# Making six of batch 1's products, and one group of tables, in an earlier step of a long-convolution and expert kernel

## The chip, the cores and the metric

The kernel runs on one core of a Trainium2 chip. The metric is the device time of one execution in microseconds. Three runs of the kernel before gave 3615.54, 3617.24 and 3617.27 us; their median, 3617.24 us, is the time before.

## What is computed

The first half is a Hyena filter: a small network gives a filter `h_filt` over 12480 positions and 128 channels, and every batch and channel of `u = x * v` is convolved with it by FFT. The second half is an expert block on every row of the result: two matrix products with `h * cos(h)` between them.

```python
h_filt = (np.maximum(pos_emb @ w1, 0.0) @ w2) * np.exp(-0.01 * pos)[:, None]
u = x * v                                  # x, v: (4, 12480, 128)
Uf = np.fft.rfft(u, n=2 * S, axis=1)
Hf = np.fft.rfft(h_filt, n=2 * S, axis=0)
y = np.fft.irfft(Uf * Hf[None], n=2 * S, axis=1)[:, :S, :]
attn = (x * y).reshape(49920, 128)
h = attn @ w_in                            # w_in: (128, 2048)
out = (h * np.cos(h)) @ w_out              # w_out: (2048, 128)
```

All inputs and outputs are float32, apart from the two expert weights, which are float64 and are converted on the chip.

## The kernel before

**The transform.** The convolution is done with matrix products: 11520 points are split as N1 = 96 times N2 = 120. For one batch there are five pieces of work, each written as a Python generator of *units*, which yields after each part of a unit, so that the pieces can be interleaved. The *products* (`u_units`) load x and v for two pairs of positions, multiply them (two instructions, L440, one for each half) and write the sum and the difference into `slots` (two instructions, L450): 30 units for a batch. The *forward step* (`f1_units`, L458 and its evictions L470) makes 64 matmul groups from `slots`. The *second step* (`f2_units`, and for the filter and batch 0 together `f2_both_units`) multiplies in the frequency domain. The *third step* (`i1_units`) makes the first half of the inverse, 64 units, each evicted from one of eight PSUM banks: mostly by an ACT copy (L562) and two DVE instructions (L564), and every eighth by an ACT copy (L555) and two POOL instructions (L558). The *last step* (`i2_units`) makes 30 groups of four positions, with a table tile `tm` for each group, multiplies by x (L586) and stores rows to `zd` in DRAM.

**The tables.** A group's tile is made by `make_group`, which calls `make_t` four times: an ACT copy with a factor (L329), another into one of two `spare` tiles (L334), and a POOL sum (L335); or, with a copy of the rows in PSUM, L329 and one DVE instruction (L331). Batch 0 makes its tiles itself and stores them in `td`, from where the later batches load them. The groups listed in `SOME` (2, 7, 12, 17, 22, 27) are made during the third step of batch 0 by `some_groups`, which also makes four sums of expert weights on POOL (L778) and at its end starts the last step, where group 0's tile is made.

**The order.** The program has two parts. Up to about 277 us the filter, batch 0's products, its forward, second and third steps run with nothing else on PE. Then the expert block runs, 98 tiles of 16 steps, and the rest of the convolution is threaded through it: `convolve` adds one step of credit for each step of the expert block and calls the generators until the credit is used up. During the last step of batch b the products of batch b + 1 are made (`inverse_units` calls `later_u_units`): L440 by POOL for one half and by DVE for the other, both L450 by POOL. Then come the forward, second and third steps of batch b + 1. The chain of the expert block for each step is PE (phase matmul, L138 `ph`), ACT (L870), DVE (L871), ACT (L876), DVE (L877); for each pair of steps POOL makes sums (L885, L888, L889), and PE multiplies by the output weights (L902).

Every engine runs its instructions in the program's order, and all DMAs of the program are issued on SP's queue, in order, each after its own waits. A tile of a pool has a number of buffers; a new tile waits until the one that had its buffer is no longer used.

The lines that matter in the third step of batch 0:

```python
with tc.tile_pool(name="ready", bufs=1) as pool:
    other = some_groups(pool)
    for i, _ in enumerate(i1_units(bank, lambda b: b % 8 == 3)):
        if i > 10 and i % 7 in (0, 3):
            next(other, None)
    for _ in other:
        pass
```

Just before this the weights (`w_in_sb`, `w_out_sb`, 1024 KB each) are loaded.

Of the kernel before, what the change touches and what calls it, by code (L numbers as in the profile page):

```python
# [10 lines left out]
F32 = mybir.dt.float32  # L11
# [3 lines left out]
ALU = mybir.AluOpType  # L15
# [19 lines left out]
def kernel(  # L35
# [46 lines left out]
    nc = tc.nc  # L82

    B, S, D = x.shape
# [3 lines left out]
    R = S // N2  # L88
    M = N1 * N2
    TURN = 4 * M  # L90
    H = N2 // 2
    ODD = 64
# [7 lines left out]
    CB = D // 2  # L100
# [5 lines left out]
    UA = 2  # L106
    NG = N2 // G
# [4 lines left out]
    ALONE = 8  # L112
    XV = 36
    LATER = 96
    AT = NFC // 2 + 2
    WCOL = 256

    dram = ctx.enter_context(tc.tile_pool(name="dram", bufs=1, space=DRAM))
# [3 lines left out]
    td = dram.tile([N2 // G, N1, G, 2, R], F32, name="td")  # L122
    wind = dram.tile([D, DFF], F32, name="wind")
    woutd = dram.tile([P, NFC // 2, 4 * CB], F32, name="woutd")
    csd = dram.tile([N2, 2, N2], F32, name="csd")
    rowsd = dram.tile([N1, 4, R], F32, name="rowsd")
    twd = dram.tile([N1, 2, N2], F32, name="twd")
# [297 lines left out]
    def clear_gap(u):  # L425

        nc.gpsimd.memset(u[:, :, H:ODD, :], 0.0)

    def u_load(place, b, a):
        tiles = []  # L430
        for i, src in enumerate((x, v)):
            tiles.append(place(a // UA, i))
            load_pairs(tiles[i], src, b, H - UA - a, H + a)
        return tiles

    def u_multiply(tiles, half, engine):
        xt, vt = (t[:, half] for t in tiles)
        if len(vt.shape) > len(xt.shape):
            xt = xt.rearrange("p (n d) -> p n d", n=UA)
        engine.tensor_tensor(xt, xt, vt, op=ALU.mult)  # L440
# [159 lines left out]

    def units(n, steps, before, mm, after, parts, ahead=2, skip=0):


        for j in range(min(ahead, n)):
            for _ in before(j) or ():
                pass
        yield 0.0
        last = iter(())  # L610
        for j in range(n):
            early = iter(before(j + ahead) or () if j + ahead < n else ())
            now = None
            for i in range(parts):
                if i == skip or 2 * (i - skip) == max(parts, 2):
                    now = mm(j, now, int(i > skip))
                if i == 0 and parts == 1:
                    now = mm(j, now, 1)
                next(last, None)
                next(early, None)  # L620
                yield steps / parts
            for _ in early:
                pass
            next(last, None)
            last = after(j, now)
        for _ in last:
            pass
        yield REST

    SOME = range(2, NG, 5)  # L630
    REST = 3.0
    U_STEPS, F1_STEPS, F2_STEPS, I1_STEPS, I2_STEPS = 2.0, 1.0, 3.4, 0.8, 1.5
    FIRST_STEPS, I2U_STEPS = 3.5, 3.4

    def u_units(b, u, engine, place, ahead, takers):

        tiles = {}

        def before(j):
            tiles[j] = u_load(place, b, j * UA)  # L640

        def after(j, _):
            for half in range(2):
                u_multiply(tiles[j], half, engine(j, half))
                yield
            if j == H // UA - 2:
                clear_gap(u)
            u_sums(u, tiles.pop(j), j * UA, takers(j))
            yield

        return units(H // UA, U_STEPS, before, lambda j, ps, i: None, after, 3, ahead=ahead)

    def later_u_units(b, u, engine, side):

        with tc.tile_pool(name="xv", bufs=3, side=side) as pool:
            def place(j, i):
                t = pool.tile([R, 2, UA * D], F32, name="xv"[i] + "t", bufs=3 - i)
                return t[:, :, :]

            yield from u_units(b, u, engine, place, 1, lambda j: (nc.gpsimd, nc.gpsimd))  # L660

    def f1_units(bank, u, share, evict=f1_evict):
        def mm(j, ps, i):
# [106 lines left out]
    def some_groups(pool):  # L770
        for g in SOME:
            t = pool.tile([N1, G, 2, R], F32, name="some", bufs=2)
            yield from make_group(pool, g, t, G)
            if g == SOME[2]:
                for dst, first_, second_, op in ((4, 1, 3, ALU.add), (5, 4, 0, ALU.subtract),
                                                 (1, 0, 1, ALU.subtract),
                                                 (6, 2, 5, ALU.subtract)):
                    nc.gpsimd.tensor_tensor(w_out_sb[:, :, dst, :], w_out_sb[:, :, first_, :],  # L778
                                            w_out_sb[:, :, second_, :], op=op)
                    yield  # L780
        next(backs[0])
# [26 lines left out]
    def inverse_units(bank, b):  # L808

        if b + 1 == B:
            yield from i2_units(bank, b, 3)
            return
        new = later_u_units(b + 1, slots[0:R, :, :, :],
                            lambda j, half: nc.vector if half else nc.gpsimd,
                            "right" if b else "left")
        parts = 4 if b == 0 else 2
        for i, steps in enumerate(i2_units(bank, b, 2)):
            if i > 2 * parts:  # L820
                for _ in range(i % parts > 0 if b == 0 else 1 + i % 2):
                    next(new, None)
            yield steps * (FIRST_STEPS if b == 0 else I2U_STEPS) / I2_STEPS
        yield from new
# [129 lines left out]
    with tc.manual_schedule():  # L954
        with tc.tile_pool(name="psum", bufs=8, space=PSUM) as psum, \
# [8 lines left out]
            parts = slots[:, :, 0:2 * N1, :].rearrange("p b (r k) i -> p r k b i", r=2)  # L964
# [87 lines left out]
            with tc.tile_pool(name="convert", bufs=1) as pool:  # L1052
                convert = convert_units(pool)
                next(convert)
                for i, _ in f1:
                    if i >= LATER and i % 9 in (0, 4):
                        if next(convert, True):
# [12 lines left out]
            for kept, here in ((rowsd, rows), (twd, tw_t)):  # L1070
# [6 lines left out]
            nc.sync.dma_start(w_out_sb[:, :, 0:4, :].rearrange("p c q d -> p c (q d)"),  # L1077
                              woutd[:, :, :])
            with tc.tile_pool(name="ready", bufs=1) as pool:
                other = some_groups(pool)  # L1080
                for i, _ in enumerate(i1_units(bank, lambda b: b % 8 == 3)):
                    if i > 10 and i % 7 in (0, 3):
                        next(other, None)
                for _ in other:
                    pass

# [39 lines left out]
        steps = [(n, c) for n in range(NALL) for c in range(NFC)]  # L1126
# [7 lines left out]
        for i in range(len(steps) + LAG):  # L1134
# [5 lines left out]
            if i < len(steps):  # L1140
                n, c = steps[i]
                if n == 0 and c == NFC // 2:
                    load(1)
                if c == (NFC - 2 if n else NFC - 1) and n + 2 < NALL:
                    load(n + 2)
                if c == AT and n > 0:
                    convolve()
                if c == AT and n - 1 in ots:
                    turned[n - 1] = moe_back(n - 1, ots.pop(n - 1))
                if c == (AT if n else NFC - 2) and n + 1 < NALL:  # L1150
                    moe_turn(mpool, n + 1)
# [10 lines left out]
            if i < len(steps):  # L1162
                if c == AT + 2 and n - 1 in obs:
                    moe_store(n - 1, obs.pop(n - 1))
            if i >= len(steps) or c != AT or n == 0:
                convolve()
# [30 lines left out]
```

## Time and profile before

| | before |
|---|---|
| median of three runs | 3617.24 us |
| time of the profiled execution | 3616.25 us |
| its span | 3614.5 us |
| granted PE clock, mean | 0.999 |
| PE busy | 3567.7 us (99%) |
| DVE, ACT, POOL busy | 78%, 62%, 76% |
| third step of batch 0 | about 222 to 277 us |
| last step of batch 0, with batch 1's products | about 277 to 530 us |

The span runs from the first to the last instruction of the profiled execution; the execution's own time is 1.75 us longer. Busy times are shares of the span. "PE" are matmuls, "PEld" loads of the stationary matrix, which overlap them. In a line of a group, a name with `<-` says which tile is written from which; after the bar come the busy time, the mean duration of one, and the idle time of the engine just before them with what ended it.

### The profile page before, as it was taken

The page shows a single profiled execution, that of the slowest core. Times are in us where ns is not written, and L with a number is a line of the kernel's source. Part 1 is how long each engine was busy: PE and PEld are TensorE (multiplying, and loading weights), DVE is VectorE, ACT ScalarE, POOL GpSimd, SP SyncE. Part 2 cuts the span into 40 slices and gives each one's busy share as a digit, 9 for nine tenths or more (in the row PEclk, how much of TensorE's full clock was granted, in tenths as well). Part 3 has the DMA queues.
Part 4 walks back from the last instruction along what each step waited for, and adds up shares of the span by engine and source line. Part 5 has one row for each costly group of instructions (what it writes and reads, how often), then busy time and mean ns, then how long its engine had stood idle before and what let it go on. Part 6 is the DMA issues. An engine that isn't in the chain of part 4 may idle for free.

```text
span 3614.5 us, 102269 instructions
## 1 busy us (share of the span) xinstructions
PE 3567.7 (99%) x40830; PEld 2533.1 (70%) x40830; DVE 2836.4 (78%) x5289; ACT 2234.2 (62%) x4482; POOL 2752.1 (76%) x3240
## 2 busy tenths in 40 slices
PE   8999999999999999999999999999999999999999
PEld 7996767666677767666677776766667776666666
DVE  7888885688887885688887786588887667877877
ACT  7776766666654556665655556665655446676676
POOL 7777985688855895698864897588885458878877
PEclk9999999999999999999999999999999999999999
DMA  6545530122214640122202551022220350000000
GB/s 189 157 147 169 159 114 16 35 72 70 70 35 130 171 134 13 31 71 72 76 26 68 171 171 47 13 65 72 74 63 15 109 153 19 19 25 19 19 23 17
DMA packets 224195, 281.85 MB, mean 78 GB/s; under 512 B 23386, under 2 KB 161122, under 8 KB 223594
## 3 DMA queue, kind: packets, MB, share of 16 engines
q1 hardware_dynamic: 223722, 275.30, 26.2%
q8 instruction: 326, 5.34, 0.6%
q14 instruction: 147, 1.20, 0.1%
HBM read 194.75 MB, written 80.46 MB: 76 GB/s over the span
## 4 chain that ended last, share of the span: by engine, by line
PE 84%; DVE 4%; POOL 2%; issue 1%; ACT 1%; DMA 0%; POOLq 0%; ACTq 0%; SPq 0%; DVEq 0%
PE ph L138 31%; PE accb L902 17%; PE cv L138 17%; PE acca L902 13%; PE cv L458 3%; DVE gt L871 1%; DVE gt L877 1%; PE ph L142 1%; PE cv L142 1%; ACT gt L870 1%; POOL ts L885 1%; POOL slots L450 0%; POOL ts L888 0%; DVE t L517 0%; DVE xt L440 0%
## 5 line engine op out<-in xcount | busy, mean ns | idle before, releaser
L871 DVE SCALAR_TENSOR_TENSOR gt<-ph,gt 128x512 f32<-128x512 f32 (+1 forms) x1380 | 948.9, 688 | 680.0 <-ACT gt L870 674.9
L870 ACT ACTIVATE gt<-ph 128x512 int32<-128x512 f32 (+1 forms) x1380 | 822.8, 596 | 1056.7 <-PE ph L138 992.6
L138 PE MATMUL ph<-at,w_in_sb 128*64 128x512 f32 (+1 forms) x5520 | 1429.0, 593 | 7.7 <-DVE gt L877 6.1
L885 POOL TENSOR_TENSOR ts<-gt 128x512 f32<-128x512 f32 (+2 forms) x784 | 1001.3, 1277 | 569.8 <-PE accb L902 565.6
L876 ACT ACTIVATE gt<-gt 128x512 f32<-128x512 f32 (+1 forms) x1568 | 972.3, 620 | 6.7 <-DVE gt L871 5.3
L877 DVE TENSOR_TENSOR gt<-ph,gt 128x512 f32<-128x512 f32 (+1 forms) x1380 | 936.6, 679 | 0.0
L902 PE MATMUL accb<-ts,w_out_sb 128*64 128x128 f32 (+2 forms) x9408 | 650.0, 272 | 0.0
L889 POOL TENSOR_TENSOR ts<-gt,ts 128x256 f32<-128x256 f32 (+2 forms) x784 | 575.7, 734 | 61.5
L888 POOL TENSOR_TENSOR ts<-ts,gt 128x256 f32<-128x256 f32 (+2 forms) x784 | 575.5, 734 | 61.4
L902 PEld LDWEIGHTS acca<-gt,w_out_sb 128*64 128x64 f32 x6272 | 395.4, 136 | 262.9 <-issue 228.6
L902 PEld LDWEIGHTS accb<-ts,w_out_sb 128*64 128x64 f32 x9408 | 543.7, 137 | 0.0
L902 PE MATMUL acca<-gt,w_out_sb 128*64 128x128 f32 (+2 forms) x6272 | 477.8, 272 | 0.0
L902 PEld LDWEIGHTS accb<-gt,w_out_sb 128*64 128x64 f32 x3136 | 221.4, 136 | 251.7 <-issue 198.7
L138 PEld LDWEIGHTS ph<-at,w_in_sb 128*64 128x64 f32 x5520 | 345.9, 137 | 37.7 <-issue 17.7
L902 PE MATMUL accb<-gt,w_out_sb 128*64 128x128 f32 (+1 forms) x3136 | 310.5, 273 | 4.9 <-DVE ot L923 3.3
L138 PEld LDWEIGHTS cv<-slots,tm 96*40 96x40 f32 (+1 forms) x3840 | 226.4, 125 | 119.5 <-issue 112.3
L902 PE MATMUL acca<-ts,w_out_sb 128*64 128x128 f32 (+1 forms) x3136 | 307.5, 272 | 1.5 <-POOL ts L888 1.4
L518 POOL TENSOR_TENSOR slots<-slots,t 120x256 f32<-120x256 f32 x288 | 210.7, 733 | 72.8 <-DVE t L517 62.0
L138 PE MATMUL cv<-slots,tm 96*40 96x128 f32 (+1 forms) x3840 | 253.0, 273 | 3.4 <-DVE slots L564 3.4
L138 PEld LDWEIGHTS cv<-even,slots 120*64 120x64 f32 (+1 forms) x3072 | 165.7, 125 | 65.0 <-issue 60.2
L902 PEld LDWEIGHTS acca<-ts,w_out_sb 128*64 128x64 f32 x3136 | 200.4, 137 | 2.5 <-POOL ts L888 2.3
L138 PE MATMUL cv<-at,w_in_sb 128*64 128x512 f32 (+1 forms) x752 | 191.7, 586 | 0.0
(140 smaller groups left out, 3834.8 us busy)
## 6 DMA issues: line engine op xcount, KB each, us to landing
h<-hd SPq DMA_DIRECT2D x144, 240.0 KB
tm<-td SPq DMA_DIRECT2D x96, 312.0 KB
xt<-in_x_dram SPq DMA_DIRECT2D x120, 208.0 KB
xs<-in_x_dram SPq DMA_DIRECT2D x120, 208.0 KB
zd<-xs SPq DMA_DIRECT2D x119, 208.0 KB
tile<-zd SPq DMA_DIRECT2D x96, 256.0 KB
vt<-in_v_dram SPq DMA_DIRECT2D x90, 208.0 KB
w<-wd SPq DMA_DIRECT2D x144, 105.0 KB
```

Of the source, the lines that this page charges most:

```text
L138: nc.tensor.matmul(dst[lo:hi], left[:, lo:hi], right, start=start, stop=stop)
L142: nc.tensor.transpose(dst, src, ident[0:n, 0:n])
L458: nc.tensor.matmul(dst[lo:hi], u[:, b, lo:hi, i], c1[0:u.shape[0], r:r + 2, :].rearrange("p r k -> p (r k)"), start=True, stop=True)
L518: nc.gpsimd.tensor_tensor(y[:, r], y[:, r], t[:, r], op=op)
L870: nc.scalar.activation(turns, ph[:, 0:m], AF.Identity, bias=phase)
L871: nc.vector.scalar_tensor_tensor(out=part, in0=ph[:, 0:m], scalar=phase, in1=turns, op0=ALU.add, op1=ALU.subtract)
L876: nc.scalar.activation(part, part, AF.Sin, scale=scale)
L877: nc.vector.tensor_tensor(part, ph, part, op=ALU.mult)
L885: nc.gpsimd.tensor_tensor(ts[:, 0:2, 0:half], gt[:, :, half:2 * half], gt[:, 0, 0:2 * half].rearrange("p (h n) -> p h n", h=2), op=ALU.sub ...
L888: nc.gpsimd.tensor_tensor(t[2], t[1], b11, op=ALU.add)
L889: nc.gpsimd.tensor_tensor(t[3], b21, t[2], op=ALU.subtract)
L902: nc.tensor.matmul(acc[h * CB:(h + 1) * CB, place, 0:r], w_out_sb[:, pair, weight, :], right[:, h * r:(h + 1) * r], start=(pair == 0 and i ...
```

## The change

Units 24 to 29 of batch 1's 30 products (`EARLY = 6`) are made in the third step of batch 0, by `early_u_units`: x and v are loaded into tiles of the pool `ready` (three buffers for x, two for v), one half is multiplied by POOL and the other by DVE, POOL makes the sum and the difference into a tile `kept`, and one call later this is stored in a new DRAM tensor `ud`. The calls are spread over the step: one at each fifth yield. In the last step of batch 0, after 24 units made as before, `kept_u_units` loads the six from `ud`, two ahead, and ACT copies them into `slots`, two instructions each. Group 0 joins `SOME`, as its first entry, so that its tile too is made in the third step, stored in `td` and loaded at the start of the last step; `some_groups` is called from i > 3 on. The first 24 units end without the three steps of rest that follow the whole set.

```diff
+    EARLY = 6
...
+    ud = dram.tile([EARLY, R, 2, CB, 2 * UA], F32, name="ud")
...
-    def units(n, steps, before, mm, after, parts, ahead=2, skip=0):
+    def units(n, steps, before, mm, after, parts, ahead=2, skip=0, rest=3.0):
...
-        yield REST
+        yield rest
...
-    SOME = range(2, NG, 5)
+    SOME = 0, *range(2, NG, 5)
...
-    def u_units(b, u, engine, place, ahead, takers):
+    def u_units(b, u, engine, place, ahead, takers, count=H // UA):
...
-        return units(H // UA, U_STEPS, before, lambda j, ps, i: None, after, 3, ahead=ahead)
+        return units(count, U_STEPS, before, lambda j, ps, i: None, after, 3, ahead=ahead,
+                     rest=REST if count == H // UA else 0.0)
+
+    def early_u_units(b, pool):
+        tiles = {}
+        def place(j, i):
+            t = pool.tile([R, 2, UA * D], F32, name="xv"[i] + "s", bufs=3 - i)
+            return t[:, :, :]
+        def before(j):
+            tiles[j] = u_load(place, b, H - (EARLY - j) * UA)
+        def after(j, _):
+            for half in range(2):
+                u_multiply(tiles[j], half, nc.vector if half else nc.gpsimd)
+                yield
+            both = tiles.pop(j)[0].rearrange("p h (n b i) -> p h n b i", n=UA, i=2)
+            kept = pool.tile([R, 2, CB, 2 * UA], F32, name="kept", bufs=2)
+            for q, op in ((0, ALU.add), (1, ALU.subtract)):
+                nc.gpsimd.tensor_tensor(
+                    kept[:, q].rearrange("p b (n i) -> p n b i", i=2),
+                    both[:, 0, ::-1, :, :], both[:, 1, :, :, :], op=op)
+            yield
+            nc.sync.dma_start(ud[j, :, :, :, :], kept[:, :, :, :])
+        return units(EARLY, 0.0, before, lambda j, ps, i: None, after, 3, ahead=1)
+
+    def kept_u_units(u, pool):
+        kept = {}
+        def before(j):
+            kept[j] = pool.tile([R, 2, CB, 2 * UA], F32, name="xt", bufs=3)
+            nc.sync.dma_start(kept[j][:, :, :, :], ud[j, :, :, :, :])
+        def after(j, _):
+            a = H - (EARLY - j) * UA
+            for q, place in enumerate((a, ODD + a)):
+                nc.scalar.copy(
+                    out=u[0:R, :, place:place + UA, :].rearrange("p b j i -> p b (j i)"),
+                    in_=kept[j][:, q])
+                yield
+            if j == EARLY - 2:
+                clear_gap(u)
+            yield
+        return units(EARLY, 0.6, before, lambda j, ps, i: None, after, 3, ahead=2)
...
-    def later_u_units(b, u, engine, side):
+    def later_u_units(b, u, engine, side, partly=False):
+        count = H // UA - (EARLY if partly else 0)
...
-            yield from u_units(b, u, engine, place, 1, lambda j: (nc.gpsimd, nc.gpsimd))
+            yield from u_units(b, u, engine, place, 1, lambda j: (nc.gpsimd, nc.gpsimd), count)
+            if partly:
+                yield from kept_u_units(u, pool)
...
-            if g == SOME[2]:
+            if g == SOME[3]:
...
-                            "right" if b else "left")
+                            "right" if b else "left", b == 0)
...
+                ahead = early_u_units(1, pool)
                 other = some_groups(pool)
                 for i, _ in enumerate(i1_units(bank, lambda b: b % 8 == 3)):
-                    if i > 10 and i % 7 in (0, 3):
+                    if i > 3 and i % 7 in (0, 3):
                         next(other, None)
+                    if i % 5 == 1:
+                        next(ahead, None)
+                for _ in ahead:
+                    pass
                 for _ in other:
                     pass
```

## The prediction, made before the changed kernel was run

> **What bounds the kernel now.** I read the page's busy shares first, then a table of stretches, then the places where TensorE (PE) stands still, then the groups and the order of time at those places. Page, part 1:
>
> ```profile
> PE 3567.7 (99%) x40830; PEld 2533.1 (70%) x40830; DVE 2836.4 (78%) x5289; ACT 2234.2 (62%) x4482; POOL 2752.1 (76%) x3240
> ```
>
> PE is idle for 3614.5 - 3567.7 = 46.8 us in all, and the change removes no matmul. So only idle PE time, or PE time at a lower clock, can be won. Stretches of 20 us (us, busy time of PE, PEld, DVE, ACT, POOL with counts, granted clock, DMA share, GB/s):
>
> ```profile
> 240.00:260.00 20.00, 20.00 (x197) 20.00 (x197) 14.68 (x43) 15.29 (x45) 14.96 (x20) 1.00 0.17 50
> 260.00:280.00 20.00, 18.47 (x199) 17.90 (x197) 13.53 (x40) 15.99 (x46) 10.82 (x18) 1.00 0.25 71
> ...
> 480.00:500.00 20.00, 19.14 (x232) 13.62 (x232) 16.70 (x29) 13.31 (x28) 18.45 (x23) 1.00 0.51 152
> 500.00:520.00 20.00, 19.72 (x215) 12.93 (x212) 16.28 (x28) 13.30 (x25) 17.71 (x21) 1.00 0.20 55
> 520.00:540.00 20.00, 17.25 (x172) 13.06 (x170) 11.49 (x19) 9.65 (x19) 17.21 (x22) 0.91 0.26 75
> ```
>
> The third step (222 to 277 us) has PE full and POOL 11 to 15 of 20; the last step of batch 0, with batch 1's products (277 to 530), has POOL at 17 to 19 of 20. At 520 to 540 PE loses 2.75 us, and the clock falls. The cause, in order of time, and in stretches of 2 us:
>
> ```profile
> 528.84 1.41 POOL L450 TENSOR_TENSOR slots<-xt 104x256 f32<-104x256 f32 x2
> 529.62 1.06 PE L458 MATMUL cv<-c,slots 104*64 104x192 f32 x3 [2.36 <-POOL slots L450]
> ```
>
> ```profile
> 530.00:532.00 2.00, 1.86 (x19) 1.70 (x20) 0.00 (x0) 0.00 (x0) 1.92 (x3) 0.67 0.22 60
> 532.00:534.00 2.00, 2.00 (x9) 1.50 (x7) 0.00 (x0) 0.00 (x0) 1.92 (x3) 0.50 0.80 207
> ```
>
> Batch 1's first forward matmul waits 2.36 us for POOL's last sums, and then runs at 0.67 and 0.50 of the clock: 2 x 0.33 + 2 x 0.50 = 1.66 us more. POOL's groups from 222 to 277 (busy us, mean ns, idle before) and the end of the third step in order of time:
>
> ```profile
> L335 POOL TENSOR_TENSOR some<-some,spare 96x208 f32<-96x208 f32 x24 | 15.0, 627 | 13.3 <-ACT spare L334 13.2
> L558 POOL TENSOR_TENSOR slots<-both 96x240 f32<-96x240 f32 x16 | 10.8, 699 | 3.7 <-ACT both L555 3.7
> L778 POOL TENSOR_TENSOR w_out_sb<-w_out_sb 128x512 f32<-128x512 f32 x4 | 5.0, 1283 | 0.0
> L335 POOL TENSOR_TENSOR tm<-tm,spare 96x208 f32<-96x208 f32 x4 | 2.5, 635 | 0.1
> ```
>
> ```profile
> 271.67 5.17 DVE L564 TENSOR_TENSOR slots<-ps,other 96x240 f32<-96x240 f32 x16 [2.14 <-ACT other L562]
> ...
> 276.99 3.08 PE L138 MATMUL cv<-slots,tm 96*64 96x128 f32 x48 [1.53 <-DVE slots L564]
> ```
>
> Here the last evictions on DVE end at 276.84 and let the last step start; PE waits 1.53 us for them, and its clock stays at 1.00.
>
> **Part by part.** Durations are from the profiled execution: span 3614.5 us, time 3616.25 us, 0.99 us below the median of 3617.24. Line numbers are those of before.
>
> *Last step, removed.* Units 24 to 29 lose one multiply and two sums on POOL each: 0.73 + 1.42 (two L450 in a row, 1.41 to 1.43) = 2.15 us, six times 12.9 us off POOL, and six multiplies off DVE. In front of 529.62 POOL's queue held units 28 and 29: L440, two L450, the memset, L440, two L450. Without these POOL is done before PE asks. The wait goes (-2.36) and with it the slow clock (-1.66), and some of the small gaps just ahead of it (0.25 at 524 to 526): **-4.4 us**. Bounds: 0, if another wait takes the place; -6, if all 2.75 us of 520 to 540, the clock and a little before it go. Elsewhere from 480 to 520 PE idles 0.86 + 0.28 = 1.1 us; I count half, -0.5, since 0.85 of it is a wait between transposes that the change leaves. Bounds 0 and -1.1.
>
> *Last step, added.* Twelve copies on ACT. The trace has no SBUF-to-SBUF copy of 104x256; the nearest rows are L329 (96x208 from SBUF, 458 ns) and L562 (96x240 from PSUM, 350). I take 460 ns, the nearer kind: 5.5 us, on an ACT that is busy 13.3 of 20 and less, so hidden as work. But the list of the changed program's instructions puts four copies in a row, two activations of the expert block, then two more. Four are 1.84 us ahead of L870 on ACT, whose result DVE's L871 and then PE wait for, while three phase banks cover about two steps of 1.8 us (eleven L876 from 500 to 520): **+0.3**, bounds 0 and +1.5. Six loads of 208 KB replace twelve in SP's queue there: nothing, at a DMA share of 0.2 to 0.5.
>
> *Third step, added.* POOL gets 12.9 us, and group 0's four sums (2.5) move forward with the others. Its work becomes 15.0 + 10.8 + 5.0 + 2.5 + 12.9 = 46.2 us; in before it worked from 226.94 to 275.37, 48.4 us. That would just fit, but can't begin evenly: unit 0's x and v (0.43 MB) stand behind 2.1 MB of weights issued at 225.6 to 226.1. DMA moved 388 GB/s from 228 to 232, 156 from 232 to 236 and 10 after that. So I put the landing at 235 (233 to 238). The list has seven POOL pieces ahead of its first multiply: 5 x 0.63 + 2 x 0.69 = 4.5 us. So 41.7 us remain from 235 on: POOL ends at 276.7, without a pause. The six DVE multiplies cost more: L440 takes 409 ns on DVE at least, 910 at the median, 2858 at most, although its size never changes, so it waits for something, and POOL is busy beside it; if each takes 0.41 us from POOL too, POOL ends at 279.2.
>
> The Trainium skill, "SBUF — State Buffer", section "SBUF: two separate sides", speaks against the change here: a GpSimd instruction and a VectorE instruction with two SBUF inputs exclude each other for a whole instruction. The spread of L440 agrees with it; by that rule the 0.41 us is paid by POOL each time (the 279.2), and without it not (the 276.7).
>
> What waits for POOL: ACT's L334 writes one of two spare buffers, so it waits for POOL's sum two before, and ACT's eviction copies (L562) stand behind it, then DVE's L564, then PE, which has eight banks of 0.83 us each (64 units from 222.3 to 275.5), less the two or three in use. After ACT's last L334 the list has six more DVE pairs. That L334 waits for a sum that has two more sums (1.25) and a pair of L558 (1.37) behind it: 276.7 - 2.6 = 274.1, or 276.6. Then 0.37 (L334) + 0.35 (L562) + 6 x 0.72 = 5.0: evictions end at 279.1 or 281.6 against 276.84, +2.3 or +4.8. I take the middle, **+3.5**. Bounds: -1.0 (group 0's eight ACT pieces no longer stand between copies at 268.4 to 271.3, and DVE was idle 2.14 us for them) and +8 (the first rival). Group 0's tile is now loaded: on SP behind the last group's store, which waits for POOL; about 2.4 to 3.6 us to land by the waits for vt (326.38) and tm (391.70), so at about 280, beside the evictions.
>
> *Clock at that border.* PE's pause grows from 1.53 us to 3 or 4. At 1.53 the clock held, at 2.36 it fell and cost 1.66. What follows is partly bound by DVE and ACT, so **+0.7**, bounds 0 and 1.7.
>
> The Trainium skill, "TensorE: Matmul & The Clock Gate", section "Part 1: The HAM clock gate", has the clock halve after an idle window of about 3.4 us at a free-running phase; by that rule this border may go either way. The trace differs in that 2.36 us sufficed at 527.3.
>
> Sum: -4.4 - 0.5 + 0.3 + 3.5 + 0.7 = **-0.4 us**: 3615.85 for the profiled execution, 3616.8 beside the median.
>
> **The rivals.**
> *The third step turns POOL-bound in earnest (slower).* Unit 0 lands at 238, three us later, and all multiplies take their toll: POOL's 41.7 + 2.5 us end at 282.2, less 2.6, plus 5.0: evictions end at 284.6, +7.8; the clock +1.7; burst +0.3; of the gain 2.4 is left, because POOL's queue in the last step starts late as well: +7.4, 3624.6 (by the median). For it: no pause in POOL for 40 us. Against it: POOL had 15 us free in this step, and DMA was nearly empty at 236. It decides when POOL's last third-step sum ends after 281.
> *The third step hides all (faster).* POOL's pieces fit into its 13.2 us of waits for spare, evictions end by 275.8 (-1.0), -4.6 at the forward step, -1.1 before it, and the border's own wait of 1.53 shrinks by 0.7: -7.4, 3609.8. Against it: the late start of unit 0.
> *The wait only changes hands.* The forward matmuls wait for ACT's copies, late behind L870 and L876 or behind a load that SP issues late: 2.4 of the 4.4 comes back, and the burst costs 1.5: -0.4 + 2.4 + 1.2 = +3.2, 3620.4. Against it: three steps of the expert block lie between the last copy and the first forward matmul.
>
> **How the numbers follow.** Forecast 0.55, POOL-bound 0.17, all hidden 0.13, handed on 0.15. A measurement of this kernel tells 0.2% (7.2 us) from no change. Faster by more: 0.13; slower by more: 0.17; within: 0.70. The sum of the bounds runs from about -8 to +11; leaving out 2 in 10 at the ends gives -6 to +8: 3611 to 3625. The likeliest case alone lies between 3613 and 3620.
>
> **What would show it.** Right: no wait of PE on POOL before batch 1's forward step and clock 1.00 there; POOL without pause from 235 to 277; the first cv matmul of the last step between 279 and 282 instead of at 276.99. Wrong: that matmul before 278 or after 284, a pause over 1 us at the forward step, or PE idle in the third step's middle by more than 2 us.

## The result and the profile after

The changed kernel takes 3622.58 us (median of 19 runs) where the kernel before takes 3617.19 us (19 runs): ratio 1.0017, 95% interval 1.0010 to 1.0023. It is 5.4 us slower; the forecast was 0.4 us faster. Three single executions of 4001 to 16289 us (one each of the kernel before, of six units alone and of the pause filled) are in the slow state and count in no ratio and no spread below. The profiled execution of after took 3622.02 us, its span is 3620.2 us, 5.7 us over that of before. In the changed kernel's code the lines have moved: L138 is now L140, L335 is L337, L440 is L442, L562 and L564 are L564 and L566, L876 is L929; the sums into `kept` are L674.

The page's busy times, then the same stretches of 20 us as shown of before, with the one in which the last step starts (us, busy PE, PEld, DVE, ACT, POOL with counts, granted clock, DMA share, GB/s):

```profile
PE 3571.1 (99%) x40830; PEld 2535.2 (70%) x40830; DVE 2829.1 (78%) x5289; ACT 2233.6 (62%) x4494; POOL 2747.3 (76%) x3240
```

```profile
240.00:260.00 20.00, 20.00 (x198) 20.00 (x197) 15.64 (x44) 13.71 (x41) 19.92 (x27) 1.00 0.51 145
260.00:280.00 20.00, 15.73 (x147) 14.96 (x145) 14.37 (x42) 14.09 (x42) 17.25 (x26) 1.00 0.35 100
280.00:300.00 20.00, 17.41 (x128) 11.74 (x130) 8.78 (x19) 9.83 (x24) 3.60 (x5) 0.66 0.43 124
480.00:500.00 20.00, 19.68 (x244) 14.06 (x242) 15.25 (x29) 13.52 (x29) 17.35 (x21) 1.00 0.51 147
...
520.00:540.00 20.00, 19.58 (x213) 13.96 (x211) 12.73 (x20) 14.70 (x32) 13.76 (x17) 1.00 0.29 75
```

The last stretch is what the change was to give: PE 19.58 instead of 17.25 and the clock at 1.00 instead of 0.91. PE is busy for as many instructions as before (40830) and 3.4 us longer in all, and idles 49.1 us instead of 46.8: most of the loss is PE running slower. The third row shows where: a clock of 0.66 over 20 us, which is 0.34 x 20 = 6.8 us of lost pulses, or 13.6 us at half clock. Before had 1.00 there. In stretches of 2 us:

```profile
280.00:282.00 2.00, 0.93 (x10) 0.96 (x12) 0.25 (x2) 1.80 (x5) 0.46 (x1) 0.60 0.70 179
...
284.00:286.00 2.00, 2.00 (x22) 2.00 (x20) 0.69 (x1) 0.00 (x0) 0.00 (x0) 0.50 0.61 161
286.00:288.00 2.00, 1.36 (x10) 0.71 (x7) 0.00 (x0) 0.51 (x1) 0.00 (x0) 0.50 0.84 242
...
292.00:294.00 2.00, 2.00 (x9) 0.62 (x8) 0.70 (x2) 1.25 (x4) 0.00 (x0) 0.50 0.01 5
294.00:296.00 2.00, 1.73 (x22) 1.01 (x18) 1.54 (x4) 1.83 (x6) 0.63 (x1) 0.98 0.00 0
```

The clock halves at the very start of the last step and is back only at 294, although PE is busy through most of it. What is ahead of it, in order of time (start, length, the engine's line; "SPq" is a DMA issue on SP's queue; in brackets the idle time and what ended it; "evictions" are the copies out of PSUM that end the third step):

```profile
276.24 3.86 DVE L566 TENSOR_TENSOR slots<-ps,other 96x240 f32<-96x240 f32 x12 [0.21 <-ACT other L564]
277.06 0.41 SPq L846 DMA_DIRECT2D tm<-td  x1
281.07 5.35 PE L140 MATMUL cv<-slots,tm 96*64 96x128 f32 x48 [4.10 <-DMA tm<-td]
```

The third step's evictions end at 276.24 + 3.86 = 280.10 (276.84 before). Group 0's tile, asked for at 277.06, ends the wait 0.97 us after that, at 281.07. PE has then stood for 4.10 us, and its 48 matmuls take 5.35 us instead of 3.08.

The two kernels have the same 1568 activations of the expert block (L876, now L929), so the n-th of one can be set against the n-th of the other (us, from the two traces; the start of before's in brackets): the first (284.58) comes 8.58 later in after, the 61st (415.8) 8.77, the 91st (485.2) 8.28, the 119th (546.1, behind the start of batch 1's forward step) 5.04, the 401st (1188.7) 4.45, the last 5.42. So the border between the third and the last step costs 8.6 us, the products and the forward step give 4.3 back by the 401st, and 1.0 comes in the remaining 2400 us. That last 1.0 can't be put down to the change: against this one execution of before, the twelve other profiles below lose 1.3 to 5.5 us there too, and none of those kernels is edited behind 550 us.

### The profile page after: what moved, and what is told of

The parts are those of the page before. It is cut to its first block, busy times and chain, and to the rows that moved or that the text cites. A ratio compares the mean times of both kernels' runs of the same rounds, so it can differ in the third digit from the quotient of the medians.

```text
span 3620.2 us, 102388 instructions
## 1 busy us (share of the span) xinstructions
PE 3571.1 (99%) x40830; PEld 2535.2 (70%) x40830; DVE 2829.1 (78%) x5289; ACT 2233.6 (62%) x4494; POOL 2747.3 (76%) x3240
## 4 chain that ended last, share of the span: by engine, by line
PE 92%; DVE 5%; ACT 1%; issue 1%; POOL 1%; DMA 1%; SPq 0%; ACTq 0%; DVEq 0%; POOLq 0%
PE ph L140 31%; PE accb L955 17%; PE cv L140 17%; PE acca L955 13%; PE cv L460 3%; PE ps L460 2%; PE ps L140 2%; PE ph L144 1%; DVE gt L924 1%; DVE gt L930 1%; PE cv L144 1%; PE ps L400 1%; ACT gt L923 1%; PE ps L496 1%; DMA tm<-td 1%
## 5 line engine op out<-in xcount | busy, mean ns | idle before, releaser
L140 PE MATMUL ph<-at,w_in_sb 128*64 128x512 f32 (+1 forms) x5520 | 1427.5, 594 | 7.3 <-DVE gt L930 5.8
L929 ACT ACTIVATE gt<-gt 128x512 f32<-128x512 f32 (+1 forms) x1568 | 972.2, 620 | 6.8 <-DVE gt L924 5.8
L140 PEld LDWEIGHTS ph<-at,w_in_sb 128*64 128x64 f32 x5520 | 344.5, 137 | 37.1 <-issue 17.9
L140 PEld LDWEIGHTS cv<-slots,tm 96*40 96x40 f32 (+1 forms) x3840 | 229.8, 126 | 125.4 <-issue 116.7
L140 PE MATMUL cv<-slots,tm 96*40 96x128 f32 (+1 forms) x3840 | 256.5, 275 | 7.4 <-DMA tm<-td 5.4
L140 PEld LDWEIGHTS cv<-even,slots 120*64 120x64 f32 (+1 forms) x3072 | 165.5, 125 | 66.6 <-issue 62.1
L140 PE MATMUL cv<-at,w_in_sb 128*64 128x512 f32 (+1 forms) x752 | 191.8, 586 | 0.0
```

Of the source, the lines that this page charges most:

```text
L140: nc.tensor.matmul(dst[lo:hi], left[:, lo:hi], right, start=start, stop=stop)
L929: nc.scalar.activation(part, part, AF.Sin, scale=scale)
```

## Experiments

Times are medians beside runs of the kernel before on the same chip (3616.78 us beside the first four kernels, 3618.35 beside the next four, 3618.77 beside the last four). "At the border" is the start of the first activation of the expert block, set against the profiled execution of before. The third step itself began at 221.5 to 222.9 us in these executions (222.31 in before), so some tenths of such a difference belong to the execution and not to the edit. A line that counts PE's matmuls shows each extra matmul of these experiments as two. The first theory was that six early units make POOL and DVE late in the third step and that the pause this leaves lets the clock fall; the rivals were group 0's tile load, and a loss in the last step.

**Group 0 alone.** The kernel before with group 0 made in the third step, no early units:

```diff
-    SOME = range(2, NG, 5)
+    SOME = 0, *range(2, NG, 5)
...
-                    if i > 10 and i % 7 in (0, 3):
+                    if i > 3 and i % 7 in (0, 3):
```

> The kernel before with group 0 alone moved into the third step (SOME with 0, some_groups from i > 3), no early units. Theory (POOL's fuller queue delays the third step, PE's longer pause there drops its clock for long, and the tile load adds about 1 us to the pause): POOL is not overfull here, so the evictions end about where they did (276 to 277.5); the load of group 0's tile, behind the last store of tables, lands about 4 us after its issue, so the last step's first matmul comes at 277 to 278.5; the clock holds if the pause stays under about 2.3 us. The forward pause of batch 1 (2.4 us and the slow clock) stays. Time -1 to +3 us against before. Rival (the load of group 0's tile is the cause of most of the loss): the last step's first matmul at 280 or later and +4 to +6 us.

3618.76 us, ratio 1.0002 (0.9993 to 1.0011). The tile is asked for at 271.29 and is never waited for; PE waits 1.44 us for DVE and starts the last step at 276.17, at full clock:

```profile
276.17 2.98 PE L138 MATMUL cv<-slots,tm 96*64 96x128 f32 x48 [1.44 <-DVE slots L564]
```

At the border it is -0.91, but 0.65 of that is the earlier start of the third step in this execution; the edit's own gain is some 0.3 us. Moving group 0 and loading its tile is not what costs.

**Six units alone.** The changed kernel without group 0 among the early ones:

```diff
-    SOME = 0, *range(2, NG, 5)
+    SOME = range(2, NG, 5)
...
-                    if i > 3 and i % 7 in (0, 3):
+                    if i > 10 and i % 7 in (0, 3):
```

> The changed kernel with the six early units, but group 0 made at its old place (SOME without 0, some_groups from i > 10). Theory (POOL queue, then the clock): evictions still end at 279 to 281, PE's pause is 3 us or more, the clock halves for one to four windows of 3.4 us, first expert activation (L876, 284.6 before, 293.2 in the changed kernel) at 289 to 293; time +2 to +5 us against before. Rival (group 0's tile load is the cause): first expert activation at 284 to 286 and a time 3 to 4 us below before, since the forward pause is gone.

3622.33 us, ratio 1.0014 (1.0005 to 1.0023): as slow as the changed kernel, without the tile's load. The start of its last step, in order of time:

```profile
277.69 5.17 DVE L566 TENSOR_TENSOR slots<-ps,other 96x240 f32<-96x240 f32 x16 [2.08 <-ACT other L564]
283.01 5.31 PE L140 MATMUL cv<-slots,tm 96*64 96x128 f32 x48 [3.41 <-DVE slots L566]
```

PE now waits for the evictions, which end at 282.86, and its matmuls are slow (5.31 us) all the same. The rival with the tile's load as the cause falls. The mix is another one, though: counted from the third step's first matmul the evictions end 2.2 us later than in after (60.47 and 58.28 us), and the slow time is shorter (table below).

**The pause filled.** The changed kernel with ten extra matmuls in the pause:

```diff
+                fill = bank()
+                for _ in range(10):
+                    nc.tensor.matmul(fill[0:N2, 0:2 * N2], cs[:, 0, :],
+                                     cs[:, :, :].rearrange("p r k -> p (r k)"),
+                                     start=True, stop=True)
```

> The changed kernel with ten extra matmuls of 120x240 on the tables in SBUF, about 4 us, put on PE between the third step's last matmul and the last step's first one; their result is not used. Theory (the clock at the border is worth about 4.5 of the 8.6 us lost there): the clock stays at 1.00, the last step's first matmul stays at about 281, the first expert activation comes at 288.5 to 289.5 instead of 293.2, and the time falls by 4 to 4.7 us against the changed kernel, to about 1 us above before. Rival (the late start after the border is due to the loads of x and v that SP issues late there, not to the clock): first expert activation at 292 to 293.5 and no change of the time.

3619.63 us, ratio 1.0006 (0.9997 to 1.0015). PE's order of time:

```profile
277.83 4.22 PE L1146 MATMUL ps<-even 120*120 120x240 f32 x20
282.81 2.90 PE L140 MATMUL cv<-slots,tm 96*64 96x128 f32 x48 [0.77 <-DMA tm<-td]
```

The third step of this execution began 0.8 and ended about 1 us later than in after, and the last step's first matmul came 1.74 us later, and yet at the border it is +5.30 instead of +8.58: the 48 matmuls take 2.90 us. Work that nobody uses, put where PE would stand, brings the expert block forward by 3.3 us in the trace; the median is 3 us below the changed kernel's, though the two intervals still overlap.

**The weights' sums on DVE.** The changed kernel with `some_groups`' four sums on DVE, 5.1 us off POOL:

```diff
-                    nc.gpsimd.tensor_tensor(w_out_sb[:, :, dst, :], w_out_sb[:, :, first_, :],
+                    nc.vector.tensor_tensor(w_out_sb[:, :, dst, :], w_out_sb[:, :, first_, :],
```

> The changed kernel with the four sums of expert weights (5.0 us on POOL in the third step) made by DVE instead. Theory (POOL's queue is what delays the third step): POOL's queue is 5 us shorter, the 4.2 us that ACT's L336 waited for POOL at 257.6 shrink below 1, evictions end at 276.5 to 278, the pause is 1 to 3 us; if the clock holds, the first expert activation is at 285 to 287 and the time 2 to 4 us below before; if it falls, 288 to 290 and about before. Rival (DVE, with six multiplies more, or the eviction chain itself is the bound): evictions end at 279 or later, as DVE now has 2 to 3 us more, and the time stays at the changed kernel's or above.

3619.18 us, ratio 1.0007 (0.9998 to 1.0016). The evictions end at 279.68, and counted from the third step's first matmul (222.19; in after 221.82) only 0.8 us earlier than in after: POOL paused again (1.05 and 0.91 us for ACT), but DVE rose to 17.56 of 20 us from 240 to 260 (15.64 in after). The trace fits a lateness of POOL and DVE together. Most of what this kernel won is clock:

```profile
280.75 4.51 PE L140 MATMUL cv<-slots,tm 96*64 96x128 f32 x48 [4.20 <-DMA tm<-td]
```

```profile
280.00:282.00 2.00, 1.25 (x14) 1.28 (x16) 0.57 (x2) 2.00 (x6) 0.62 (x1) 0.77 0.59 157
...
284.00:286.00 2.00, 1.77 (x22) 1.39 (x18) 0.69 (x1) 0.14 (x1) 0.00 (x0) 0.88 0.59 165
```

The pause is as long as after's (4.20 and 4.10 us), but the slow time is 3.4 us and not 13.7. So the pause's length alone does not set it.

**Three units.** The changed kernel with one number changed:

```diff
-    EARLY = 6
+    EARLY = 3
```

> The changed kernel with EARLY = 3: three units are made early instead of six. Theory (the third step's lateness is a backlog of POOL and DVE work that grows faster than the number of units): in the run with group 0 alone POOL still waited some 13 us for spare tiles, and three units add 6.5 us, so the evictions end at 276.2 to 277.5 instead of 280.1 and the last step starts by 278 at full clock. 6.5 us off POOL's queue in front of the forward step is still more than the 2.36 us that PE waited, so the whole -4.6 us there stays, and the burst of copies on ACT costs +0.7 instead of +1.3. Sum -0.9 - 0.3 + 0.7 - 4.6 = -5: about 3612. Rival (each early unit costs the third step its share, 4.0 us for six in the evictions' end): +2.0 there, a pause of 3 us, half a window or more of slow clock, and -4 at the forward step: about 3616 to 3617.

3616.11 us, ratio 0.9996 (0.9988 to 1.0005); 6.5 us below the changed kernel's median.

```profile
272.83 4.19 DVE L566 TENSOR_TENSOR slots<-ps,other 96x240 f32<-96x240 f32 x12 [0.21 <-ACT other L564]
277.73 4.51 PE L140 MATMUL cv<-slots,tm 96*64 96x128 f32 x48 [1.89 <-DMA tm<-td]
```

Evictions end at 277.02. From the third step's first matmul that is 54.33 us (before 54.53, group 0 alone 54.26, after 58.28): the first three units cost next to nothing, the next three 3.95. The theory's backlog holds and the rival's equal shares fall. Its "full clock" was wrong, and with it the 2.3 us that the first experiment's expectation allowed a pause: 1.89 us, here by the tile, was enough for one slow stretch of 3.4 us (+1.77 at the border). At the forward step the wait is gone as with six, and by the 401st activation it is 1.69 us ahead of before; it did not keep that (below).

**The tile loaded earlier.** The changed kernel with `next(backs[0])`, which issues those loads, moved ahead of the last group of `SOME`:

```diff
         for g in SOME:
+            if g == SOME[-1]:
+                next(backs[0])
...
-        next(backs[0])
```

> The changed kernel with one move: the loads that open the last step (group 0's tile and its x) are issued before the last of the early groups is made, some 4 us earlier on SP's queue, so that the tile is there when the evictions end. Theory (the pause is set by the evictions, and its length only decides how the clock falls): evictions still end at about 280.1, the first product of the last step at 280.2 instead of 281.07, so -0.9 us, a pause of 3.2 instead of 4.1 us, and a slow time that is still there in most executions but shorter: 3619 to 3621 against 3622.6. Rival (the tile's load is the cause of the slow clock): no slow clock at that border, -0.9 and -4.5: about 3617.

3621.29 us, ratio 1.0009 (1.0000 to 1.0018); 3622.58 for the changed kernel.

```profile
279.92 5.35 PE L140 MATMUL cv<-slots,tm 96*64 96x128 f32 x48 [3.39 <-DVE slots L566]
```

The wait goes over to the evictions, the last step's first matmul is 1.15 us earlier (0.33 of it because the whole third step began earlier in this execution), and the slow time has its 13.7 us unshortened (0.72 over 24 us). The tile was worth 0.8 us and nothing of the clock; that the slow time would be shorter was wrong.

**The forward step's pause filled.** The kernel before with six extra matmuls ahead of batch 1's forward step:

```diff
+        if back is backs[1]:
+            fill = bank()
+            for _ in range(6):
+                nc.tensor.matmul(fill[0:N1, 0:2 * N1], c1[0:R, 0, :],
+                                 c1[0:R, 0:2, :].rearrange("p r k -> p (r k)"),
+                                 start=True, stop=True)
```

> The kernel before with six extra matmuls of 104x96 by 104x192 (0.35 us each) on a table of cosines, just ahead of batch 1's forward step, where PE waits 2.36 us for POOL; their results are not used. Theory (the wait and the slow clock after it are two costs, 2.36 and 1.7): POOL still releases the first forward matmul at about 529.6, but the clock stays at 1.00 there: -1.7 us in the executions that had a slow time, about 3615.5. Rival (the slow clock there costs nothing, since POOL and DVE go on being behind): no difference, 3617.

3616.16 us, ratio 0.9996 (0.9987 to 1.0005).

```profile
526.80 2.19 PE L833 MATMUL cv<-c 104*96 104x192 f32 x12
529.23 1.06 PE L458 MATMUL cv<-c,slots 104*64 104x192 f32 x3 [0.24 <-POOL slots L450]
```

```profile
530.00:532.00 2.00, 2.00 (x24) 1.79 (x26) 0.00 (x0) 0.00 (x0) 1.84 (x3) 1.00 0.46 83
```

POOL still releases PE as late, 0.39 us ahead of before as was everything earlier in this execution; behind it the lead is 2.07. So the slow clock there costs 1.68 us, and the wait is the rest: the two costs that the prediction summed are separate. The median is 2.2 us below that of before on the same chip, which the interval does not tell from nothing.

**Three units and the earlier tile.** The changed kernel with both edits:

```diff
-    EARLY = 6
+    EARLY = 3
...
+            if g == SOME[-1]:
+                next(backs[0])
```

> EARLY = 3 together with the early loads of the last step's first tile. If the evictions set the start of the last step with three units (theory), this is the same as EARLY = 3 alone within 0.5 us, about 3612. If the tile's load sets it (rival), it is some 1 to 4 us faster than EARLY = 3 alone.

3616.22 us, ratio 0.9997 (0.9988 to 1.0005), the same as three units alone. PE's wait is 1.96 us and now ends with the evictions; the slow stretch is again 3.4 us, +1.18 at the border. The lead expected over before, 5 us, did not show in the median of either kernel with three units.

**Three units, earlier tile, pause filled.** As the last, with four matmuls of 120x120 by 120x240 in the pause:

```diff
+                fill = bank()
+                for _ in range(4):
+                    nc.tensor.matmul(fill[0:N2, 0:2 * N2], cs[:, 0, :],
...
```

> Three early units, the early loads of the last step's first tile, and four extra matmuls of 120x120 by 120x240 (0.42 us each, their results not used) between the third step's last product and the last step's first, where PE paused 1.96 us. Theory (pause and slow clock are two costs): the pause stays, the clock stays at 1.00, and of the +1.2 us at that border some 1.5 go: -0.3; -3.7 over the products' end and the forward step, as with three units before: -4.0, about 3613 where the kernel before takes 3617. Rival (the extra matmuls only take the pause's place, and what follows is late all the same because DVE and ACT are behind): no difference from three units without them, 3616.

3616.28 us, ratio 0.9994 (0.9985 to 1.0002). At the border it is +0.36 (expected -0.3), and at the 301st activation 3.28 us ahead of before. Then it loses what it had, far from the change:

```profile
2041.85 1.26 PE L140 MATMUL cv<-slots,tm 96*64 96x128 f32 x16 [2.03 <-DMA tm<-td]
```

A later batch's last step waits 2.03 us for its table and pays a slow stretch behind it; four of the fourteen profiles have a wait of 1.5 to 2.5 us at that place (the three kernels with three units, and six units with the pause filled), the others 0 to 0.7. Whether that is chance or follows from the shifted times was not settled. It is one reason why a lead of 3 us in the trace is no clear gain in the medians; another is that the profiled execution of before is a quick one behind the 401st activation, as said above.

**Group 0 and the filled forward step.** The kernel before with two of the edits above:

```diff
-    SOME = range(2, NG, 5)
+    SOME = 0, *range(2, NG, 5)
...
+            for _ in range(6):
+                nc.tensor.matmul(fill[0:N1, 0:2 * N1], c1[0:R, 0, :],
```

> The kernel before with group 0 in SOME (made in the third step, from i > 3 on) and the six extra matmuls ahead of batch 1's forward step (0.35 us each, results not used); no unit is made early. If the effects add: -0.9 us at the third step's end and -1.7 us by the clock at the forward step, while the wait of 2.36 us for POOL stays: -2.6, about 3614.6. Rival (they do not add, since POOL's work for group 0 moves the other waits): -1 to -2.

3616.51 us, ratio 0.9994 (0.9985 to 1.0002). At the border it is -0.60 (0.39 of it an earlier start of the third step), at the 119th activation, behind the forward step's start, -2.33, and at the 401st -2.37. In the trace the two add, with 0.2 us for group 0 instead of the 0.9 expected and 1.7 for the filled pause; the medians can't tell.

**Six units, earlier tile, pause filled.** The kernel with the earlier tile and seven extra matmuls:

```diff
+                fill = bank()
+                for _ in range(7):
+                    nc.tensor.matmul(fill[0:N2, 0:2 * N2], cs[:, 0, :],
...
```

> The changed kernel (six early units) with the early loads of the last step's first tile and seven extra matmuls of 120x120 by 120x240 (2.95 us, results not used) in the pause of 3.4 us before the last step. Theory: evictions end at about 280 as before, the clock stays at 1.00, the first activation of the expert block comes 3.1 us later than in the kernel before instead of 7.4 to 8.6, and with -4.2 at the products' end and the forward step the whole is -1.1: about 3616 to 3617, with executions closer to each other than the changed kernel's. Rival (the late start costs as much without the slow clock): 3620 or more.

3618.34 us, ratio 0.9999 (0.9990 to 1.0008).

```profile
277.61 3.00 PE L1147 MATMUL ps<-even 120*120 120x240 f32 x14
281.17 2.99 PE L140 MATMUL cv<-slots,tm 96*64 96x128 f32 x48 [0.56 <-DVE slots L566]
```

The evictions end at 280.91, counted from the third step's first matmul as late as in after (58.22 and 58.28 us), and PE starts the last step 0.10 us later than there; but at the border it is +4.10 instead of +8.58, and by the 401st activation -0.06. All six units, all of the lateness, without the slow clock: no difference from before. Beside it on the same chip, the changed kernel again (next) takes 6.0 us more by the median, of which the earlier tile explains 0.8. This is the experiment that settles the loss.

**The changed kernel again,** with no edit.

> The changed kernel once more, unaltered, for a second profiled execution. If the length of the slow clock is a matter of chance (the phase at which the pause falls), this profile shows another length than 13.65 us, a multiple of 3.41 us, and the first activation of the expert block comes earlier or later by about half the difference. If it is fixed by what follows the pause, it is 13.65 us again.

3624.34 us, ratio 1.0014 (1.0006 to 1.0023).

```profile
282.54 5.35 PE L140 MATMUL cv<-slots,tm 96*64 96x128 f32 x48 [4.28 <-DMA tm<-td]
```

```profile
276.00:300.00 24.00, 17.75 (x147) 12.93 (x145) 13.12 (x34) 12.53 (x32) 6.25 (x10) 0.79 0.45 124
```

0.21 x 24 = 5.0 us of pulses, or 10.1 us at half clock, against 13.6 in the first profile of the same program (0.72 over these 24 us). The slow time differs between executions of one kernel. The spread of the times fits this: from lowest to highest 7.2 and 7.5 us for the changed kernel and 4.7 to 7.5 us for the other kernels without extra matmuls, but 2.4 to 4.0 us for the five kernels with them.

The next table is from the traces. In every profile the times between the changes of the clock, from 3.41 us to over 3600, are multiples of 3.41 us; a *clock window* is one such stretch of 3.41 us, and the windows lie at another place in each execution. The third column is PE's busy share in the window that holds the greatest part of the pause, which is also the window at whose end the clock fell where it did.

| kernel | PE's pause, us | PE busy in that window | slow time, us | clock falls, from the last step's first matmul | first matmul to first activation, us |
|---|---|---|---|---|---|
| three units, filled | 0.21 | 94% | 0 | | 7.55 |
| six units, early tile, filled | 0.56 | 84% | 0 | | 7.51 |
| the pause filled | 0.77 | 78% | 0 | | 7.07 |
| group 0 alone | 1.44 | 58% | 0 | | 7.50 |
| before | 1.53 | 55% | 0 | | 7.59 |
| three units | 1.89 | 45% | 3.4 | 0.9 after | 8.62 |
| three units, early tile | 1.96 | 43% | 3.4 | 0.2 after | 8.66 |
| weights' sums on DVE | 4.20 | 9% | 3.4 | 0.3 after | 8.63 |
| six units alone | 3.41 | 30% | 6.8 | 1.7 ahead | 9.44 |
| changed kernel again | 4.28 | 0% | 10.2 | 0.2 ahead | 11.36 |
| changed kernel | 4.10 | 0% | 13.7 | 0.7 ahead | 12.09 |
| early tile | 3.39 | 11% | 13.7 | 0.4 ahead | 12.08 |

## Why the prediction was wrong, step by step

**What failed: "Clock at that border".** The term was +0.7 with a bound of 1.7, sized by the forward step of before, where one fall cost 1.66 us. It measured 12.09 - 7.59 = **4.5 us**, which takes the sum from -0.4 to +3.4. The mechanism was named, the pause was foreseen ("grows from 1.53 us to 3 or 4", measured 4.10), and only the size was off: I took the price of one fall as the price of any. The table shows the difference. Where the clock fell after the last step's first matmul, PE was busy through the whole first slow window, and the clock came back at its end, 3.4 us later. Where it fell in the pause, the first slow window still held a part of the pause (PE busy for 50 to 94% of it), and the clock stayed low for 6.8 to 13.7 us. So the price, 1.0 to 4.5 us in the last column, hung in part on where the pause lay among the clock windows, and these lie differently in each execution.

Breaks in the work at this border may be what then keeps the clock down: in after PE waits 0.64 us for ACT at 287.3, which is the 1.36 of 2.00 in 286 to 288. That is a reading and not shown, and one window speaks against it: from 283.83 to 287.25 the profile of after has PE busy without a break, and the clock stayed at half all the same. What sets the length beyond the first slow window is open. That the length varies from one execution to the next, and that filling the pause takes all of it away, is shown.

The Trainium skill, "TensorE: Matmul & The Clock Gate", section "Part 1: The HAM clock gate", says that full clock comes back after a sustained busy window of about 3.4 us. The slow times here, 3.4, 6.8, 10.2 and 13.7 us, are multiples of that window, but the window of after from 283.83 to 287.25 does not fit. Its idle window of the same length before a fall does not fit either: 1.89 us of pause sufficed here, in a window in which PE was busy for 45% of the time.

**A small miss: the tile's load.** The prediction put it "at about 280, beside the evictions" and so gave it no time of its own. It landed at about 281, which cost 0.97 us; loading it earlier took 0.8 us off.

**Right: the third step.** The first early multiply ran at 235.09, as estimated (235), and POOL then did not pause until 275.4, where it waited 0.69 us for ACT:

```profile
235.09 0.97 POOL L442 TENSOR_TENSOR xs<-xs,vs 104x256 f32<-104x256 f32 x1 [1.23 <-DMA vs<-in_v_dram]
```

The evictions end +3.26 us later; against the step's own start, which was 0.49 us earlier in after, it is +3.75, for a forecast of +3.5. POOL's groups from 222 to 280 (busy us, mean ns, idle before) show the toll that was left open between 0 and 2.5 us, that is, how much longer POOL's instructions take beside a busier DVE:

```profile
L337 POOL TENSOR_TENSOR some<-some,spare 96x208 f32<-96x208 f32 x28 | 17.9, 651 | 5.3 <-ACT spare L336 5.3
...
L674 POOL TENSOR_TENSOR kept<-xs 104x256 f32<-104x256 f32 x12 | 8.9, 757 | 0.1
...
L442 POOL TENSOR_TENSOR xs<-xs,vs 104x256 f32<-104x256 f32 x6 | 5.0, 827 | 1.2 <-DMA vs<-in_v_dram 1.2
```

Against 627, 710 and 730 ns, the durations that the prediction took from before, it is 28 x 0.024 + 12 x 0.047 + 6 x 0.097 = 1.8 us. That DVE is what lengthens them was not tested by itself.

**Right: the forward step and the products.** No wait of PE on POOL over 0.2 us there, and the clock at 1.00:

```profile
530.00:532.00 2.00, 2.00 (x20) 1.18 (x18) 1.67 (x3) 1.44 (x3) 1.84 (x3) 1.00 0.57 132
532.00:534.00 2.00, 2.00 (x28) 1.70 (x26) 1.73 (x4) 1.12 (x2) 0.59 (x2) 1.00 0.88 237
```

The terms -4.4, -0.5 and +0.3 make -4.6; from the 61st to the 401st activation it is -4.3. From 480 to 500 PE's idle time fell from 0.86 to 0.32 us: the wait between transposes, 0.85 us, which the prediction took the change to leave, shrank to 0.31. The burst of copies on ACT cost PE no wait over 0.21 us.

**The sum again with what was measured.** -0.49 (earlier start) + 3.75 (evictions) + 0.97 (tile) - 0.15 (what PE waited past the evictions in before) + 4.50 (clock) = 8.58; -4.3; +1.0 behind the 401st activation, which no edit here explains: 5.3 against 5.42 at the last activation. Against the forecast of -0.4 that is 5.8 us too slow, of which the clock is 3.8, the start of the last step 0.6 (4.08 for 3.5), the products and the forward step 0.3, and the end 1.0.

**The rivals.** "POOL-bound in earnest" gave nearly the right time (3624.6) by a way that was not taken: it needed POOL's last sum after 281, which was at 278.4, and evictions at 284.6. "Hides all" fails by the evictions. "Changes hands" fails: PE waits for no copy of ACT. And the signs under "Right" in what would show it came true, with 281.07 inside 279 to 282 and POOL's first pause at 275.4 instead of 277, while the forecast was wrong: the signs at this border ended at the last step's first matmul, and the loss came in the 12 us behind it.

## What to carry to other kernels

Price a pause of PE by the slow clock that can follow it too: here a pause of 4.10 us was followed by 13.7 us at half clock, which cost 4.5 us more, and in another execution of the same kernel by 10.2 us. Where work is moved into a step with slack, find out how much it takes before the slack is gone: three units cost the third step next to nothing here, six did not fit. A few matmuls that nobody uses, put into a pause that can't be removed, are a cheap test of what the clock costs, and here a cure; still, no version was shown to beat the kernel before, the best two standing at 0.9994 with intervals from 0.9985 to 1.0002.

## What the runs showed of the hardware that was not expected

After pauses of about the same length (4.10, 4.20, 4.28 us) the clock stayed at half for 13.7, 3.4 and 10.2 us. A pause of 1.53 us at this border cost no clock, one of 1.89 us did. What separates them in these traces is the busy share of one clock window of 3.41 us. Apart from the last 10 us of the program, the clock fell eleven times in the fourteen profiles, each time at the end of a window in which PE was busy for 45% or less, and no window with 53% or more was followed by a fall; none lay between. In seven of the eleven the first slow window was busy throughout, and the clock came back at its end (3.4 us); in the other four it held part of the pause, and the clock stayed low for longer. While the clock was at half from 282 to 286 the profile has PE busy for 2.00 of every 2.00 us: a busy share does not tell a slow engine from a full one, and only the granted clock beside it does.
